# Attention in chunks of 128 tokens, two heads at a time, one chunk shared by both, its probabilities split into two narrow parts; U and V narrowed during the MLP

## The chip, the cores and the metric

The kernel runs on one core of a Trainium2 chip. Its time is the device time of one execution in microseconds (us). The core has a matrix engine (TensorE, PE; its loads of stationary operands are listed as PEld), a vector engine (VectorE, DVE), an activation engine (ScalarE, ACT), a general one (GpSimd, POOL), a queue engine that issues most transfers (SyncE, SP) and sixteen DMA engines. Program order is fixed on each engine ahead of the run; an engine waits where an instruction needs something that another engine or a transfer has not delivered.

## The reference

Four batches of 448 tokens go through three stages. Everything is float32.

```
q_n, k_n = rmsnorm(q, g_q), rmsnorm(k, g_k)          # q, k, v: (4, 12, 448, 64)
attn = softmax(q_n @ k_n.T / 8);  o = attn @ v        # per batch and head
x = o.transpose(0, 2, 1, 3).reshape(4, 448, 768)
xn = layernorm(x) * g_ln
x = x + relu(xn @ w1a) @ w2a                          # 768 -> 3072 -> 768
u = x + (x.T @ U @ V).T                               # U: 448x32, V: 32x448
out = u + relu(u @ w1b) @ w2b
```

## The kernel before

Attention takes the first 335 us, the two MLP passes the rest. The time of the MLP passes is nearly all products that follow one another on PE, in an order written by a planner with costs of its own (`mlps`); smaller work is put between them as side tasks.

Attention works on 48 heads (batch times head), in 24 pairs; n is a head and pr = n // 2 its pair. A head's 448 tokens are four chunks of 112 (CP = 112, NC = 4): a tile of q or k has 112 partitions, and 8 chunks of 64 numbers for the pair. Products keep float32 accuracy by splitting an operand into a narrow high part and the narrow rest: k into k_hi and k_lo, side by side in `kk`; q into q_hi, twice side by side in `qd`, and q_lo in `ql`, which has room for two more columns.

A score is then the sum of two products with the keys of a chunk as the stationary operand: `a1` (k_hi over k_lo, 128 rows) with `bq` (q_hi over q_hi), L503; and `a2` (k_hi, and rows of ones) with `t` (q_lo, and a row with minus the maximum), L504. `a2` needs k_hi on partitions 0 to 63 beside its rows of ones, so a DMA copies a1's upper half into it (L459, the transfer a<-a of the trace). Generators hold the stages of a head:

- `pre_load`, `pre`, `pre_v`, by pair: SP loads q and k (L240); squares and casts on ACT (L290, L316, L319), row sums on DVE (L299), scaling and the low parts on POOL (L297, L313, L318, L321); v comes by ACT's queue.
- `t1` (L438, L448): PE transposes k and q, four blocks each, results pk and pq; ACT casts them into a1 and bq.
- `mx` (L459 to L471): the copy into a2; four products pm, whose row maxima DVE takes (L464); ACT writes minus the maximum into ql.
- `t2` (L479, L481): PE transposes ql, result pt; ACT casts it into t.
- `sc` (L503 to L506): per chunk the two products into one bank ps, and ACT's exponential p. For some chunks p is split (`part`): DVE rounds it to a high part (L494), POOL subtracts (L495).
- `pv` (L521 to L526): p times v with a column of ones, one float32 product of two passes per chunk, or three narrow products where p was split. In all 24 chunks are split, those of heads 6 to 17: chunks 0 and 1.
- `norm` (L535 to L539): DVE copies the sum out, SP writes it to x and the denominators to a scratch.

The main loop has a step per head. In step i it goes round-robin over sc of head i, mx of i + 2, pv of i − 1, t1 of i + 3, t2 of i + 1 and norm of i − 2, four rounds a step, one piece of each per round. A second list (pre, pre_v, layer norm of finished batches, narrowing of the first weights, and at step 4 `load_uv`, which narrows U and V from 64-bit inputs) goes forward by a piece a round. From this order the scheduler fixes each engine's program and the waits. a1 and bq have four buffers by head; a2 has three, taken in turn by head:

```python
a2 = a2s[n % NA2]                                    # before, in t1; NA2 = 3
nc.sync.dma_start(f32(a2[0:D, :]), f32(a1[0:D, :]))  # in mx
```

So the copy for head i + 2 goes into the buffer that head i − 1 read in the step before.

Of the kernel before, what the change touches and what calls it, by code (L numbers as in the profile page):

```python
# [18 lines left out]
P = 128  # L19
CP = 112  # L20
NC = S // CP
DM = H * D
# [11 lines left out]
H0, H2, H1, NV = 6, 18, 18, 2  # L34
# [3 lines left out]
PVY = (0, 1, 2)  # L38
NL = 2
NA2 = 3  # L40
# [7 lines left out]
def build(tc, qkv, gg, g_ln, w1a, w2a, w1b, w2b, u_in, v_in, out):  # L48
    nc = tc.nc
    V, A, PL, PE = nc.vector, nc.scalar, nc.gpsimd, nc.tensor  # L50
    with ExitStack() as es:
# [52 lines left out]
        u4 = const([CP, NC, 4 * R], F32R, "u4")  # L104
        v4 = const([4 * R, S], F32R, "v4")

        def load_ggt(tp):
            gsb = x[B - 1][:CP, 0, :2 * D].rearrange("p (j d) -> p j d", j=2)
            nc.scalar.dma_start(gsb, gg)
            ggt = tp.tile([CP, D], F32, tag="ggt", name="ggt")  # L110
            V.scalar_tensor_tensor(ggt, gsb[:, 0, :], 1.0 / D ** 0.5, gsb[:, 1, :], ALU.mult, ALU.mult)
            return ggt

        def load_uv():
            for src, n, rows in ((u_in, NC * 4 * R, CP), (v_in, S, 4 * R)):
                f = fpool.tile([rows, n], F32, tag="wf", name=f"f{n}")
                src = src.bitcast(U32).rearrange("p (n t) -> p n t", t=2)
                parts = []
                for i in range(2):
                    r = rpool.tile([rows, n // 2, 2], U32, tag="raw", name=f"r{n}_{i}")  # L120
                    nc.sync.dma_start(r, src[:, i * n // 2:(i + 1) * n // 2])
                    parts.append(r)
                yield
                narrow(parts, f)
                yield
                if rows == CP:
                    V.tensor_copy(u4.rearrange("p c r -> p (c r)"), f)
                    part = u4[:, :, 2 * R:3 * R]
                    V.tensor_tensor(part, f.rearrange("p (c r) -> p c r", c=NC)[:, :, 2 * R:3 * R], f32(part), ALU.subtract)
# [96 lines left out]
        def attention(ap, ep, ep2, early, late):  # L226
            NH = B * H
            NP = NH // 2
            kks, vfs, vhs, vls, a2s = [], [], [], [], []
            st = {}  # L230

            def pre_load(pr):
                if pr < NP:
                    b, hp = divmod(pr, H // 2)
                    st["raw", pr] = raw = []
                    for a in range(2):
                        pool, tag, n = ((rpool, "raw", 4), (ap, "rawk", 4))[a]
                        raw.append(pool.tile([CP, 2 * NC, D], F32, tag=tag, name=f"raw{pr}_{a}", bufs=n))
                        q = nc.scalar if pr + a == 0 else nc.sync
                        ins = q.dma_start(raw[a], qkv[b, hp, :, a])  # L240
# [6 lines left out]
            identr = ap.tile([CP, CP], F32R, tag="identr", name="identr")  # L247
            pin(V.tensor_copy(identr, ident[:CP, :CP]))
# [3 lines left out]
            later = ap.tile([CP, D], F32, tag="later", name="later")  # L252
# [180 lines left out]
            def t1(n):  # L433
# [8 lines left out]
                if n == 0:  # L442
                    pin(ins)
# [1124 lines left out]
```

## Time and profile before

| | |
|---|---|
| time, median of 3 runs | 1674.63 us (1674.07 to 1676.15) |
| the profiled execution: its time, its span | 1671.72 us, 1669.6 us |
| PE busy in the span | 1657.2 us (99%) |
| DVE, ACT, POOL busy in the span | 1218.3, 1001.3, 1081.3 us |
| granted PE clock | full (1.0) in every slice |
| attention | 0 to 335 us, the MLP passes from there on |

A busy PE here means that a product is under way by the profile, so a table by stretches tells more than the sum: whether PE has idle time in the stretch, and how much the others have. The chain of waits is followed back from the last instruction, each step to what released it. A group is all instructions of one line, one engine, one pair of tiles.

### The profile page before, as it was taken

What the parts mean: (1) busy time and instruction counts of PE and PEld (TensorE: products, weight loads), DVE (VectorE), ACT (ScalarE), POOL (GpSimd) and SP (SyncE); (2) the same over time, 40 slices, a digit from 0 to 9 for tenths busy, and PEclk for the clock granted to TensorE, in tenths of its full rate; (3) what the DMA queues carried; (4) which work ended last, traced back from release to release, by engine and by line L of the source; (5) the groups of instructions that cost most, each with busy time, mean ns of one, the idle gap of its engine ahead of it and who ended that gap; (6) DMA issues with size and microseconds to landing.
All of it is one profiled execution on the core that took longest, in us unless ns stands there. A gap on an engine that the chain in (4) does not pass through costs nothing.

```text
span 1669.6 us, 24779 instructions
## 1 busy us (share of the span) xinstructions
PE 1657.2 (99%) x8247; PEld 1439.5 (86%) x8247; DVE 1218.3 (73%) x1937; ACT 1001.3 (60%) x2104; POOL 1081.3 (65%) x958
## 2 busy tenths in 40 slices
PE   8999999999999999999999999999999999999999
PEld 6676666599999999999999999999999999999998
DVE  6788787979887887867767786667667854565665
ACT  7887888767878875644544455444445534454541
POOL 5788676459758687755555687555455555776752
PEclk9999999999999999999999999999999999999999
DMA  4444445667665656543544427565757464444432
GB/s 112 114 105 101 131 115 146 195 220 218 217 199 163 193 191 214 183 142 125 160 135 163 158 86 254 192 215 175 225 192 255 157 208 123 144 150 124 152 123 76
DMA packets 134432, 273.42 MB, mean 164 GB/s; under 512 B 37280, under 2 KB 57664, under 8 KB 134304
## 3 DMA queue, kind: packets, MB, share of 16 engines
q1 hardware_dynamic: 112252, 265.24, 50.0%
q10 hardware_dynamic: 22052, 6.59, 1.7%
q8 instruction: 66, 1.08, 0.3%
q14 instruction: 62, 0.51, 0.1%
HBM read 178.80 MB, written 81.96 MB: 156 GB/s over the span
## 4 chain that ended last, share of the span: by engine, by line
PE 92%; DVE 2%; POOL 2%; issue 2%; DMA 1%; ACT 0%; SPq 0%; POOLq 0%; DVEq 0%; ACTq 0%
PE bank L1170 34%; PE bank L1348 32%; PE bank L1292 6%; PE po L521 5%; PE b L1170 3%; PE ps L503 2%; PE b L1292 2%; PE ps L504 2%; PE pm L463 2%; PE b L1348 1%; PE t L1037 1%; PE xt L1027 1%; DVE m L464 1%; PE pk L438 1%; PE pq L448 1%
## 5 line engine op out<-in xcount | busy, mean ns | idle before, releaser
L1348 PE MATMUL bank<-h,w 128*128 128x448 f32 x2607 | 576.0, 366 | 0.0
L1348 PEld LDWEIGHTS bank<-h,w 128*128 128x128 f32 x2607 | 488.4, 188 | 38.4 <-issue 0.4
L1359 DVE TENSOR_TENSOR x<-x,bank 128x448 f32<-128x448 f32 x442 | 270.8, 616 | 189.4 <-PE bank L1348 184.8
L1170 PE MATMUL bank<-xh,w 128*128 128x448 f32 x1122 | 320.2, 367 | 0.0
L844 POOL TENSOR_TENSOR w<-wf,w 128x384 fp32r<-128x384 f32 x201 | 222.7, 1119 | 133.7 <-ACT w L843 132.8
L844 POOL TENSOR_TENSOR w<-s,w 128x384 fp32r<-128x384 f32 x151 | 173.5, 1152 | 154.0 <-ACT w L843 144.0
L1170 PE MATMUL bank<-T,w 128*128 128x448 f32 x1134 | 251.9, 367 | 0.0
L1170 PEld LDWEIGHTS bank<-T,w 128*128 128x128 f32 x1134 | 212.0, 188 | 16.7
L1170 PEld LDWEIGHTS bank<-xh,w 128*128 128x128 f32 x1122 | 210.1, 188 | 17.5 <-issue 0.8
L1170 PE MATMUL bank<-xl,w 128*128 128x448 f32 x561 | 205.1, 366 | 0.0
L843 ACT CAST w<-s 128x384 fp32r<-128x384 f32 x151 | 77.2, 516 | 175.9 <-PE bank L1170 160.9
L843 ACT CAST w<-wf 128x384 fp32r<-128x384 f32 x201 | 101.3, 514 | 100.9 <-PE bank L1170 82.0
L521 PE MATMUL po<-p,vf 112*66 112x448 f32 x336 | 153.2, 539 | 0.6 <-DVE m L464 0.6
L464 DVE TENSOR_REDUCE m<-pm 112x1 f32<-112x448 f32 x192 | 117.8, 617 | 41.3 <-PE pm L463 40.4
L83 DVE SCALAR_TENSOR_TENSOR wf<-wf,raw 128x384 uint32<-128x384 uint32 x180 | 134.9, 756 | 13.7 <-ACT raw L71 5.8
L844 POOL TENSOR_TENSOR w<-raw,w 128x384 fp32r<-128x384 f32 x72 | 81.1, 1143 | 57.4 <-ACT w L843 57.3
L79 ACT ACTIVATE wf<-raw 128x384 f32<-128x384 f32 x180 | 99.1, 552 | 27.9 <-DMA raw<-in_w2a 11.0
L1170 PEld LDWEIGHTS bank<-xl,w 128*128 128x128 f32 x561 | 105.4, 188 | 8.4
L506 ACT ACTIVATE p<-ps 112x448 f32<-112x448 f32 x192 | 104.3, 545 | 4.2 <-PE ps L504 1.9
L1162 DVE SCALAR_TENSOR_TENSOR h<-tm,h 128x448 fp32r<-128x448 f32 x103 | 101.6, 986 | 4.6 <-ACT h L1161 3.8
L71 ACT ACTIVATE raw<-raw 128x384 uint32<-128x384 uint8 x180 | 99.9, 557 | 0.0
L1211 DVE TENSOR_TENSOR tm<-tm,bank 128x448 f32<-128x448 f32 x99 | 61.1, 617 | 44.7 <-PE bank L1170 44.0
(285 smaller groups left out, 3023.8 us busy)
## 6 DMA issues: line engine op xcount, KB each, us to landing
wd<-wf SPq DMA_DIRECT2D x94, 384.0 KB
ws<-w SPq DMA_DIRECT2D x84, 384.0 KB
w<-ws SPq DMA_DIRECT2D x84, 384.0 KB
wf<-wd SPq DMA_DIRECT2D x51, 384.0 KB
raw<-wd SPq DMA_DIRECT2D x48, 384.0 KB
raw<-in_w1b SPq DMA_DIRECT2D x48, 384.0 KB
raw<-in_w2b SPq DMA_DIRECT2D x48, 384.0 KB
raw<-in_w2a SPq DMA_DIRECT2D x44, 384.0 KB
```

What stands on the lines that cost most here:

```text
L71: A.activation(r[:, :, 0], r.bitcast(U8).rearrange("p n (t q) -> p n t q", t=2)[:, :, 0, 3], AF.Copy, scale=1.0 / 32, bias=-31.0 / 64)
L83: V.scalar_tensor_tensor(f, f, 3, r[:, :, 0], ALU.logical_shift_left, ALU.bitwise_or)
L464: ins = V.tensor_reduce(m[:, c:c + 1], pm[:CP, :S], AX.X, ALU.max)
L506: A.activation(p, pb[:CP, :S], AF.Exp)
L521: PE.matmul(po[:QW, :S], vf[:, j, c, :], ps[c], start=(i == 0), stop=(i == NC - 1))
L843: job(A, 520, lambda: A.copy(form(key)[0], src()), ins, ("hi",) + key, [key])
L844: job(PL, 1100, lambda: PL.tensor_tensor(form(key)[1], src(), f32(form(key)[0]), ALU.subtract), [("hi",) + key], key, rel=rel)
L1162: soon(V, 700, lambda: V.scalar_tensor_tensor(at(*key)[:, 1], src(), 0.0, f32(at(*key)[:, 0]), ALU.max, ALU.subtract), [("hh",) + key], ke ...
L1170: PE.matmul(out[:, :S], wt[:, k, :], xt[:, k, :], start=(first and n == 0), stop=(last and n == 8), skip_group_check=True)
L1292: PE.matmul(at(*to)[:, :S], wt[:, e, :], xt, start=(m in "13" and n == 0), stop=(n == 2), skip_group_check=True)
L1348: PE.matmul(at(*key)[:, :S], wt[:, e % 3, :], t, start=(n == 0), stop=(n == 3 * G - 1))
L1359: V.tensor_tensor(x[b][:, e, :], x[b][:, e, :], at(*key)[:, :S], ALU.add)
```

## The change

The 896 tokens of a head pair are seven chunks of 128 (PC = 7). Chunks 0 to 2 are the first head's, 4 to 6 the second's, and chunk 3 holds the last 64 tokens of the first and the first 64 of the second. For chunk 3 the tiles a1, bq and a2 have 64 columns of zeros between the two heads' columns, so that its keys can be taken with the other half zero; its maxima (pm) and its scores (ps) are two products that accumulate in one bank, one for each head, and its p is exponentiated once. A second input layout `vv` holds v in eight slots, the two of the shared chunk with the other head's half zeroed. What was counted by head is now counted by pair, with these numbers before and after: transposes of k and q 384 and 336, of ql 192 and 168; products pm 192 and 192, score products 384 and 384; exponentials 192 and 168; maxima 192 and 168; float32 products of p with v 168 and 140; groups of three narrow ones 24 and 52. Chunk 3 is split in pairs 2 to 21, chunks 2 and 4 also in pairs 3 to 8; the split of chunk 3 is made once and used in a group of three for either head. DVE has 24 copies of 64 columns more, ACT 24 more, POOL 24 small memsets more at the start.

Buffers: a1 has two and bq three, by pair; t has two, by pair, the second in the tile that later holds U and V. Of a2, the first heads of the pairs have two buffers in turn, and all second (odd) heads one, `a2s[1]`, named a21 in the order.

`load_uv` is no longer in attention: it is a side task in the first MLP pass, in three pieces.

The order of the work changes with the pairs. On PE, in a step of an odd head, the last products of attention's rounds; a21 and a22 are buffers of a2 (numbers behind names are those of the tiles), ps, pm, pk and po banks. Before, head 29, with its buffer a22:

```order
L503 MATMUL ps365_3099<-bq_29_2899,a1_29_2850 112x448 [waits Activation_49]
L504 MATMUL ps365_3099<-t2_29_3050,a22_364 112x448 [waits DMAHW2_49]
L463 MATMUL pm366_3106<-a1_31_3026,bq_31_3072 112x448 [waits Activation_49]
L521 MATMUL po367_3109<-p28_0_3012,vf0_348 66x448 [waits DMAHW5_49,DVE_49]
L438 MATMUL pk368_3111<-identr_309,kk16_3007 128x112 [waits PE_49,Pool_49]
L438 MATMUL pk368_3111<-identr_309,kk16_3007 128x112 x3
L503 MATMUL ps369_3127<-bq_29_2899,a1_29_2850 112x448 [waits Activation_49]
L504 MATMUL ps369_3127<-t2_29_3050,a22_364 112x448
L463 MATMUL pm370_3132<-a1_31_3026,bq_31_3072 112x448 [waits DVE_49]
L521 MATMUL po367_3109<-p28_1_3039,vf0_348 66x448
L479 MATMUL pt2371_3136<-identr_309,ql0_366 66x112 [waits DVE_49,Activation_49]
```

After, head 35, from the shared chunk's score on (L558 and L559 are the two score products there, L492 in SP's list the copy):

```order
L558 MATMUL ps400_3414<-bq2_374,a11_368 128x448
L559 MATMUL ps400_3414<-uv0_386,a21_379 128x448 [waits Activation_49]
L507 MATMUL pm401_3417<-a10_366,bq0_370 128x448
L475 MATMUL pk402_3438<-identr_307,kk19_3345 128x128 [waits DVE_49,Pool_49]
L475 MATMUL pk402_3438<-identr_307,kk19_3345 128x128 x3
L558 MATMUL ps403_3451<-bq2_374,a11_368 128x448 [waits PE_49]
L513 MATMUL pm404_3456<-a10_366,bq0_370 128x448 [waits Activation_49]
L596 MATMUL po405_3459<-p17_0_3351,vf1_356 66x448 [waits DMAHW2_49,PE_49]
L558 MATMUL ps406_3468<-bq2_374,a11_368 128x448 [waits DVE_49]
L513 MATMUL pm407_3473<-a10_366,bq0_370 128x448 [waits Activation_49]
L596 MATMUL po405_3459<-p17_1_3377,vf1_356 66x448
L559 MATMUL ps403_3451<-uv0_386,a21_379 128x448 [waits DMAHW3_49]
```

Before, the first product with a22 waits for the copy that was issued in an earlier step, and the later ones for nothing more. Now the second product in this piece is the last of the shared chunk; the last row waits for a transfer into the same a21, and the products and transposes between them are what was moved ahead of it.

On SP, near the end of attention, where wr are first weights and xn, x and sum results. Before:

```order
L980 DMA wr00_4604<-in_w1a 128x768 [waits DMAHW1_49,Pool_49]
L459 DMA a22_364<-a1_41_3893 64x448 [waits DMAHW2_49,PE_49,Activation_49]
L212 DMA xn1_91<-ln1_d5_3903 128x448 [waits DMAHW3_49,DVE_49]
L538 DMA x3_85<-u37_3994 64x448 [waits DMAHW4_49,DVE_49]
L539 DMA sum3_3895<-u37_3994 1x448 [waits DMAHW5_49]
L980 DMA wr01_4606<-in_w1a 128x768 [waits DMAHW6_49,Pool_49]
L459 DMA a20_360<-a1_42_3992 64x448 [waits DMAHW1_49,PE_49,Activation_49]
```

After:

```order
L218 DMA xn1_89<-ln1_d4_3678 128x448 [waits DMAHW5_49,DVE_49]
L1065 DMA wr01_4385<-in_w1a 128x768 [waits DMAHW6_49,Pool_49]
L492 DMA a21_379<-a10_366 64x448 [waits DMAHW7_49,PE_49]
L218 DMA xn1_89<-ln1_d5_3710 128x448 [waits DMAHW0_49,DVE_49]
L625 DMA x3_83<-u37_3794 64x448 [waits DMAHW1_49,DVE_49]
L626 DMA sum3_3729<-u37_3794 1x448 [waits DMAHW3_49]
L492 DMA a22_382<-a11_368 64x448 [waits DMAHW4_49,Activation_49]
```

In both the copies stand between weight loads and results. The copy into a21 after the change waits for PE in its own step, and its source a10 is that of the next pair.

In the program `sc` of head i comes first in a round and `mx` of head i + 2 second, and `mx` issues the copy in its first round. With the one buffer of odd heads the copy for the next pair comes behind the read of chunk 3 and ahead of the reads of chunks 4 to 6, which therefore take the next pair's k_hi in the product with q_lo.

The diff, cut to the parts that are spoken of:

```diff
-H0, H2, H1, NV = 6, 18, 18, 2
+C0, C1, X0, X1 = 2, 22, 3, 9
...
-NA2 = 3
...
         def load_uv():
...
+            t = both()
+            u4, v4 = t[:CP, S:].rearrange("p (c r) -> p c r", c=NC), t[:, :S]
+            uv.extend([u4, v4])
+            for src, rows, at, n in ((u_in, CP, 0, 2 * P), (u_in, CP, 2 * P, 2 * P), (v_in, P, 0, S)):
...
+                    r = lpool.tile([rows, n // 2, 2], U32, tag="lt", name=f"r{rows}_{at}_{i}")
+                    nc.sync.dma_start(r, src[:, at + i * n // 2:at + (i + 1) * n // 2])
+                    raws.append(r)
+                for _ in range(3):
+                    yield
+                narrow(raws, f)
                 yield
...
+            def halved(pr):
+                return (2, 3, 4) if X0 <= pr < X1 else (3,) if C0 <= pr < C1 else ()
...
+            a1s, bqs, a2s, t2s = [], [], [], []
+            for lst, nm, n in ((a1s, "a1", 2), (bqs, "bq", 3)):
+                for i in range(n):
+                    t = ep2.tile([P, 2 * S + HC], F32R, tag=f"{nm}{i}", name=f"{nm}{i}")
+                    PL.memset(f32(t[:, S:S + HC]), 0.0)
+                    lst.append(t)
+            for i, j in enumerate((0, 1, 0)):
+                t = ap.tile([P, S + HC], F32R, tag=f"a2{i}", name=f"a2{i}")
                 PL.memset(f32(t[D:QW, :]), 1.0)
+                PL.memset(f32(t[:QW, 0:HC] if j else t[:QW, S:]), 0.0)
                 a2s.append(t)
+            t2s.append(ap.tile([P, 2 * S], F32R, tag="t2", name="t2"))
+            t2s.append(both())
             qls = []
...
+            def a2_of(n):
+                pr, j = divmod(n, 2)
+                return a2s[1] if j else a2s[2 * (pr % 2)]
+
+            def cols(n):
+                o = n % 2 * (S + HC)
+                return slice(o, o + S)
+
+            def keys(c, j):
+                o = c * P if c < 3 or not j else c * P + HC
+                return slice(o, o + P)
...
-                a2 = a2s[n % NA2]
-                st["ab", n] = (a1, bq, a2)
+                if not j:
+                    st["ab", pr] = (a1s[pr % 2], bqs[pr % 3])
+                cs = range(NC) if not j else range(NC, PC)
+                for nm, src, t in (("pk", kk, st["ab", pr][0]), ("pq", qd, st["ab", pr][1])):
+                    pt = bank(nm)
+                    for c in cs:
+                        o = (c - cs[0]) * P
+                        PE.transpose(pt[:, o:o + P].bitcast(F32R), src[:, c].rearrange("p a d -> p (a d)"), identr)
+                    hold = pin if n == 0 or nm == "pq" and n in (1, 3) else lambda ins: ins
+                    if not j:
+                        hold(A.copy(t[:, 0:S], pt[:, :S]))
+                        hold((A.copy if nm == "pk" else V.tensor_copy)(t[:, S + HC:S + P], pt[:, S:S + HC]))
+                    else:
+                        hold(A.copy(t[:, S + P:2 * S + HC], pt[:, 0:S - HC]))
+                    if nm == "pk":
+                        yield
...
             def mx(n):
-                a1, bq, a2 = st["ab", n]
-                nc.sync.dma_start(f32(a2[0:D, :]), f32(a1[0:D, :]))
-                m = ap.tile([CP, NC], F32, tag="m", name=f"m{n}", bufs=2)
-                for c in range(NC):
-                    pm = bank("pm")
-                    PE.matmul(pm[:CP, :S], bq[:, c * CP:(c + 1) * CP], a1, start=True, stop=True)
-                    ins = V.tensor_reduce(m[:, c:c + 1], pm[:CP, :S], AX.X, ALU.max)
+                pr, j = divmod(n, 2)
+                a1, bq = st["ab", pr]
+                ql = st["tok", pr][1]
+                a2 = a2_of(n)
+                to = slice(HC, S + HC) if j else slice(0, S)
+                nc.sync.dma_start(f32(a2[0:D, to]), f32(a1[0:D, cols(n)]))
+                if not j:
+                    st["m", pr] = ap.tile([P, PC], F32, tag="m", name=f"m{pr}", bufs=2)
+                m = st["m", pr]
+
+                def top(c, pm):
+                    ins = V.tensor_reduce(m[:, c:c + 1], pm[:, :S], AX.X, ALU.max)
                     if n == 2:
                         pin(ins)
-                    if c < NC - 1:
+
+                def turned(c, d):
+                    A.mul(ql[:, c:d, D:D + 1], m[:, c:d].unsqueeze(2), -1.0)
+
+                if j:
+                    pm = st.pop(("pm", pr))
+                    PE.matmul(pm[:, :S], bq[:, keys(3, 1)], a1[:, cols(n)], start=False, stop=True)
+                    top(3, pm)
+                    turned(0, NC)
+                    yield
+                for c in range(NC, PC) if j else range(3):
+                    pm = bank("pm")
+                    PE.matmul(pm[:, :S], bq[:, keys(c, j)], a1[:, cols(n)], start=True, stop=True)
+                    top(c, pm)
+                    if c < PC - 1:
                         yield
-                pr, j = divmod(n, 2)
-                ql = st["tok", pr][1]
-                A.mul(ql[:, j * NC:(j + 1) * NC, D:D + 1], m.unsqueeze(2), -1.0)
+                if j:
+                    turned(NC, PC)
+                else:
+                    st["pm", pr] = pm = bank("pm")
+                    PE.matmul(pm[:, :S], bq[:, keys(3, 0)], a1[:, cols(n)], start=True, stop=False)
 
...
             def sc(n):
-                a1, bq, a2 = st.pop(("ab", n))
-                t = st.pop(("t2", n))
-                st["p", n] = ps = []
-                st["hl", n] = hl = []
+                pr, j = divmod(n, 2)
+                a1, bq = st["ab", pr]
+                a2, t = a2_of(n), t2s[pr % 2]
+                t = t[:QW, j * S:(j + 1) * S]
...
+                def score(pb, c, start=True, stop=True):
+                    k = keys(c, j)
+                    o = k.start - j * S
+                    PE.matmul(pb[:, :S], a1[:, k], bq[:, cols(n)], start=start, stop=False)
+                    PE.matmul(pb[:, :S], a2[:QW, o:o + P], t, start=False, stop=stop)
+
+                def expd(pb, c):
+                    ps[c] = p = ap.tile([P, S], F32, tag="pf", name=f"p{pr}_{c}", bufs=NC + 2)
+                    A.activation(p, pb[:, :S], AF.Exp)
+
+                if j:
+                    part(2)
+                    pb = st.pop(("pb", pr))
+                    score(pb, 3, start=False)
+                    expd(pb, 3)
+                    yield
+                for c in range(NC, PC) if j else range(3):
+                    if c in (5, 6):
+                        part({5: 3, 6: 4}[c])
                     pb = bank("ps")
-                    cs = slice(c * CP, (c + 1) * CP)
-                    PE.matmul(pb[:CP, :S], a1[:, cs], bq, start=True, stop=False)
-                    PE.matmul(pb[:CP, :S], a2[:QW, cs], t[:QW], start=False, stop=True)
-                    p = ap.tile([CP, S], F32, tag="pf", name=f"p{n}_{c}", bufs=NC + 2)
-                    A.activation(p, pb[:CP, :S], AF.Exp)
-                    ps.append(p)
-                    if c < NC - 1:
+                    score(pb, c)
+                    expd(pb, c)
+                    if c < PC - 1:
                         yield
+                if not j:
+                    st["pb", pr] = pb = bank("ps")
+                    score(pb, 3, stop=False)
 
...
-                    if c >= m:
-                        PE.matmul(po[:QW, :S], vf[:, j, c, :], ps[c], start=(i == 0), stop=(i == NC - 1))
+
+                def times(po, s, c, first, last):
+                    if c in hl:
+                        ph, pl = hl[c]
+                        w = s - 2
+                        PE.matmul(po[:QW, :S], vh[:, w, :], ph, start=first, stop=False)
+                        PE.matmul(po[:QW, :S], vl[:, w, :], ph, start=False, stop=False)
+                        PE.matmul(po[:QW, :S], vh[:, w, :], pl, start=False, stop=last)
                     else:
-                        ph, pl = hl[c]
-                        PE.matmul(po[:QW, :S], vh[:, j, c, :], ph, start=False, stop=False)
-                        PE.matmul(po[:QW, :S], vl[:, j, c, :], ph, start=False, stop=False)
-                        PE.matmul(po[:QW, :S], vh[:, j, c, :], pl, start=False, stop=(i == NC - 1))
-                    if i in PVY:
+                        PE.matmul(po[:QW, :S], vf[:, s, :], ps[c], start=first, stop=last)
+
...
-                if i == 4:
-                    ln.append(load_uv())
...
+                if (layer, pair, c) == (0, 1, 2):
+                    side.append((even, 4, "uv", load_uv()))
...
+    vv[:, :, :, :NC - 1] = v[:, :, :, :NC - 1]
+    vv[:, :, :HC, NC - 1] = v[:, :, :HC, NC - 1]
+    vv[:, :, HC:, NC] = v[:, :, HC:, NC - 1]
+    vv[:, :, :, NC + 1:] = v[:, :, :, NC:]
```

## Rows read from the trace of the kernel before

**Rows 1.** Stretches; us; busy us (count) PE, PEld, DVE, ACT, POOL; clock; DMA; GB/s.
```profile
0.00:40.00 40.00, 35.57 (x209) 26.59 (x209) 27.82 (x60) 29.59 (x71) 20.00 (x33) 1.00 0.43 113
40.00:335.00 295.00, 290.55 (x1436) 182.63 (x1435) 236.78 (x448) 244.16 (x574) 209.81 (x178) 1.00 0.49 130
335.00:668.00 333.00, 333.00 (x1642) 307.94 (x1641) 280.67 (x390) 250.86 (x484) 248.01 (x206) 1.00 0.64 201
700.00:750.00 50.00, 50.00 (x256) 46.30 (x255) 33.19 (x53) 26.00 (x54) 29.29 (x27) 1.00 0.48 153
```

**Rows 2.** Chain of waits, steady attention: start us, us, engine, result, line, count.
```profile
59.17 0.29 PE pk L438 x4
59.46 0.27 PE ps L503
59.73 0.21 PE ps L504
59.93 0.20 PE pm L463
60.14 0.75 PE po L521 x2
60.89 0.22 PE pt L479 x4
61.11 0.26 PE ps L503
```

**Rows 3.** Time line of PE in a split chunk: start us, us, instruction.
```profile
81.90 0.37 PE L524 MATMUL po<-xl,vh 112*66 112x448 f32 x1
82.10 0.36 PE L525 MATMUL po<-xl,vl 112*66 112x448 f32 x1
82.30 0.36 PE L526 MATMUL po<-xl,vh 112*66 112x448 f32 x1
82.50 0.36 PE L503 MATMUL ps<-bq,a 128*112 128x448 f32 x1
```

**Rows 4.** Groups, 40 to 335 us: shapes, count; busy us, mean ns; idle before.
```profile
L464 DVE TENSOR_REDUCE m<-pm 112x1 f32<-112x448 f32 x171 | 105.3, 617 | 38.0 <-PE pm L463 37.2
L506 ACT ACTIVATE p<-ps 112x448 f32<-112x448 f32 x179 | 97.5, 546 | 4.2 <-PE ps L504 1.9 <-PE pm L463 0.9 <-ACT ln_mu L172 0.5
...
L504 PEld LDWEIGHTS ps<-t,a 66*112 66x112 f32 x178 | 31.5, 177 | 8.7 <-issue 4.6 <-ACT p L506 1.0 <-ACT t L481 0.8
...
L495 POOL TENSOR_TENSOR xh<-p,xh 112x448 fp32r<-112x448 f32 x12 | 14.1, 1180 | 1.9 <-DVE xh L494 0.7 <-DVE ss L301 0.6 <-DVE ln L148 0.4
...
L494 DVE TENSOR_REDUCE xh<-p 112x448 fp32r<-112x448 f32 x12 | 7.3, 611 | 1.4 <-ACT p L506 1.4
```

**Rows 5.** Page, groups of the whole span: the MLP's loads of 128 columns.
```profile
L1348 PEld LDWEIGHTS bank<-h,w 128*128 128x128 f32 x2607 | 488.4, 188 | 38.4 <-issue 0.4
```

**Rows 6.** Time line of POOL at the start; in brackets its idle time before.
```profile
3.07 0.21 POOL L278 MEMSET ql<- 112x16 f32 x3
6.05 1.28 POOL L380 TENSOR_TENSOR raw<-raw,ggt 112x512 f32<-112x512 f32 x1 [2.76 <-DVE identr L248]
...
15.46 1.04 POOL L362 TENSOR_TENSOR raw<-raw,sy 112x512 f32<-112x512 f32 x1 [1.41 <-DVE sy L149]
...
20.01 1.27 POOL L297 TENSOR_TENSOR raw<-raw,later 112x512 f32<-112x512 f32 x1
```

**Rows 7.** Time line of SP: issues of the copy for the second score product.
```profile
81.92 0.47 SPq L459 DMA_DIRECT2D a<-a  x1
...
88.09 0.46 SPq L459 DMA_DIRECT2D a<-a  x1
```

**Rows 8.** DMA, 81.9 to 85.9 us in 40 slices: busy share in tenths.
```profile
DMA  0000000000055998520000100000003698893000
```

**Rows 9.** Chain of waits in attention's tail: the two longest transfers.
```profile
284.95 3.75 DMA a<-a
...
303.94 6.16 DMA wr<-in_w2a
```

More of the change, by code (lines that the diff above doesn't have):

```diff
@@ L296, in pre @@
                     yield
-                pin(PL.tensor_tensor(raw[0], raw[0], over(later, [CP, n8, D], 1), ALU.mult))
+                pin(PL.tensor_tensor(raw[0], raw[0], over(later, [P, n8, D], 1), ALU.mult))
                 for a in range(2):
@@ L318, in pre @@
                 PL.tensor_tensor(kk[:, :, 1, :], raw[1], f32(kk[:, :, 0, :]), ALU.subtract)
-                pin(A.copy(qd, over(raw[0], [CP, n8, 2, D], 2)))
+                pin(A.copy(qd, over(raw[0], [P, n8, 2, D], 2)))
                 yield
@@ L368, in high @@
                     else:
-                        pin(A.copy(qd, over(raw[pr][0], [CP, n8, 2, D], 2)))
+                        pin(A.copy(qd, over(raw[pr][0], [P, n8, 2, D], 2)))
                 def low(E, pr, a):
@@ L396, in first_two @@
                 low(PL, 0, 0)
-                pin(PL.tensor_tensor(raw[1][0], raw[1][0], over(later, [CP, n8, D], 1), ALU.mult))
+                pin(PL.tensor_tensor(raw[1][0], raw[1][0], over(later, [P, n8, D], 1), ALU.mult))
                 pre_load(3)
@@ L475, in t2 @@
                 ql = st["tok", pr][1]
+                t = t2s[pr % 2]
                 yield
+                if not j:
+                    yield
                 pq = bank("pt2")
-                for c in range(NC):
-                    PE.transpose(pq[:QW, c * CP:(c + 1) * CP].bitcast(F32R), ql[:, j * NC + c], identr)
-                t = ap.tile([P, S], F32R, tag="t2", name=f"t2_{n}", bufs=T2 + 1)
-                ins = A.copy(t[:QW], pq[:QW, :S])
+                cs = range(NC) if not j else range(NC, PC)
@@ new lines, in pv @@
+                if not j:
+                    if n:
+                        yield
+                    po = st["po", n] = bank("po")
+                    for c in range(3):
+                        times(po, c, c, c == 0, False)
+                        if c < 2:
+                            yield
+                else:
+                    times(st["po", n - 1], 3, 3, False, True)
+                    po = st["po", n] = bank("po")
+                    times(po, 4, 3, True, False)
+                    order = (5, 6, 4) if 4 in hl else (4, 5, 6)
+                    for i, c in enumerate(order):
+                        yield
+                        times(po, c + 1, c, False, i == 2)
```

179 lines of the change are left out of this document (82 added, 97 removed).

## The prediction

> **What bounds the kernel now.** I read the table by stretches first. TensorE (PE) is busy 290.55 us of the 295 from 40 to 335 us, the attention after its start, and 333.00 of 333 and 50.00 of 50 in the two stretches of the MLPs, at full granted clock (2.4 GHz) everywhere [rows 1]. What PE is spared in attention therefore shortens the program, and what another engine is spared shows only as far as PE waits for it: 40.00 − 35.57 = 4.43 us before 40 us and 295 − 290.55 = 4.45 after. The other engines have room: DVE 236.78, ACT 244.16, POOL 209.81 of the 295. In the chain of waits the products of a round then follow one another [rows 2]: a product in one pass starts 0.20 us after the one before, a product of p with v 0.75 (F32, two passes), and a block of four transposes 0.29 or 0.22, after which the next product takes 0.26 or 0.27 instead of 0.20.
>
> **The sum, part by part.**
>
> *More p split.* In place of one F32 product a split chunk has three narrow ones. In the row of a split chunk the first starts at 81.90 us and the product after the third at 82.50, so 0.60 [rows 3], against 0.75. The change has 52 groups of three instead of 24: a shared chunk's split serves a product for either head (20 pairs × 2), and six pairs have two more. So 28 × (−0.15) = −4.2 us. Chunks that are split number 32 instead of 24, each with a DVE pass of 0.611 and a POOL pass of 1.18 us [rows 4]: +4.9 on DVE, +9.4 on POOL. Against that DVE has 24 maxima fewer of 0.617 (−14.8), ACT 24 exponentials fewer of 0.546 (−13.1) [rows 4], and POOL's token work 448 columns a partition instead of 512. No engine beside PE gets fuller, so I put the cover at whole. What it costs if it isn't: a split that comes 0.2 late in each of 32 chunks would be +6.
>
> *Fewer transposes.* k and q have seven blocks a pair instead of eight, with 128 columns instead of 112: 336 for 384, and 168 for 192 of the third kind. A block of four pk costs 0.29 plus the 0.06 to 0.07 that the next product is late, so 0.35, or 0.088 each; of pt 0.22 + 0.05 = 0.27, or 0.067 [rows 2]. If an instruction costs the same at 128 columns: 48 × 0.088 = 4.2 us less for k and q, and 24 × 0.067 = 1.6 for the third kind. If the cost goes by columns, 7 × 128 = 8 × 112 and nothing is won. The pk blocks (128 rows of result) and the pt blocks (66) have the same moving columns and unlike times, so columns alone don't set it. I take −4.2: k and q by instruction, the third kind by column. Bounds −5.8 and 0.
>
> *As many products as before.* Maxima and scores: the shared chunk has one product per head into one bank, so 8 a pair of either, 192 and 192 + 192 as before, and 192 chunks of p with v. They now load 128 stationary columns where there were 112. The load of 112 columns takes 177 ns and that of 128 in the MLP 188 [rows 4, 5], both under the 0.20 at which products start, so I put it at 0. The Trainium skill, "TensorE: Matmul & The Clock Gate", section "LDWEIGHTS (loading the stationary operand)", has a load grow with its columns; here the rows agree in the sign, but 66 columns [rows 3], 112 [rows 2] and 128 (333.00 / 1642 = 0.203 in the MLP [rows 1]) go by at the same pace, which leaves the load hidden. Were it not hidden, the 576 products would pay 11 ns each, the fourth rival.
>
> *Start.* The first chain runs through POOL and ACT: instructions of 1.28, 1.04 and 1.27 us on 512 columns [rows 6]. With 448 an eighth goes: about six of them, 6 × 1.2 × 0.125 = −0.9; I take −0.8. There are 24 small memsets more on POOL, of some 0.1 us by the 3 × 0.07 of the row at 3.07 us, so 2.4 us, and POOL waits 2.76 us before its first real work at 6.05, which hides them; uncovered they'd cost up to 2.2. Bounds −1.5 and +2.2.
>
> *U and V narrowed later.* In attention this takes DVE, ACT, POOL work and four SP loads away and so, with the relief above, part of PE's 4.45 us of idle: −1, bounds −4.45 and 0. In the MLPs the same work stands beside a PE at 50.00 of 50 with DVE at 33.19 and ACT at 26.00 [rows 1]; the MLP's products stand in the same order as before. I put it at 0; if h is late once for each of its pieces, three to six waits under 0.8 us, up to +5.
>
> *The wait that is new.* Head n's second score product reads k_hi from a copy (a<-a) on partitions 0–63. Before, three buffers went round by head, the copy was issued two steps ahead and had a step (6.2 us, the distance of the copies issued at 81.92 and 88.09 us [rows 7]) to land. Now all odd heads have one buffer, and the copy for the next odd head stands, in the program, behind only the first read of this one. So PE's chunk-4 product waits for the landing of a copy that was released in the same step, by chunk 3's product. Behind that product on PE: chunk 5's, eight transposes, the score of chunk 6, and ACT's exponentials and casts wait for these. The work between release and wait, from the order and the durations above: pm 0.20, four pk 0.355, ps 0.20, pm 0.20, po 0.76, ps 0.20, pm 0.20, po 0.76 = 2.88 us. A product ends 0.37 after its start [rows 3], 0.17 beyond the 0.20 that is counted for it, and the two hand-overs to and from the queue I estimate at 0.09 together, so 2.62 are left from issue to landing. The copy issued at 81.92 [rows 7] has its packets on the queues from 83.0 to 83.7, so lands some 1.8 to 2.2 after issue [rows 8]. Margin 0.4: no stall while the queues are quiet. But in the tail the copy took 3.75 us, and a 384-KB load 6.16 [rows 9]. In SP's order the copies of the last four pairs stand behind weight loads or a string of normalised rows. I price those four at 3.75 − 2.62 = 1.13, rounded up for the 6.16 to 1.25 each: +5. Bounds 0 (all land in 2.2) and 4 × (6.16 − 2.62) = +14.
>
> The Trainium skill, "DMA: Bandwidth & Descriptors", section "Issuing engines are not separate DMA queues", says that transfers share the same 16 engines and interleave, whoever issues them. The rows on the tail copy agree (3.75 us against about 2), and it is what speaks against this change: the margin is only as good as the quiet of the queues.
>
> Sum: −4.2 − 4.2 − 0.8 − 1 + 5 = −5.2 us. Against the profiled execution (1671.72 us around a span of 1669.6) that is 1666.5. The median of the runs shown is 1674.63, 2.9 above that execution, so I carry the difference over: **1669.6 us** after rounding the difference to −5. About 0.2%, 3.35 us, is what a measurement of this kernel can tell from none.
>
> **Rivals.**
>
> *A, slower: every pair's copy is late.* The copy lands later than 2.62 us because x and sum of the even head (SP L538, L539 before) and the next raw loads are under way. Two pairs have longer cover, 22 pay. Without stalls the sum is −10.2, so it turns slower than before from 10.2 / 22 = 0.46 us a pair, a landing at 3.08. At 3.3: 22 × 0.68 = +15, so +4.8, 1679.4. For it: the loaded 3.75. Against: rows 8 show the quiet case in mid-attention, with 0.4 of margin.
>
> *B, no change: transposes by column, the tail stalls.* −4.2 (splits) − 0.8 − 1 + 5 = −1: 1673.6. For it: the same moving data in fewer blocks. Against: the pk and pt blocks above.
>
> *C, clearly faster: no stalls.* −10.2: 1664.4. For it: the tail's PE had waits of its own already (the stretch lacks 4.45 us in all), and a late copy may coincide with one of these. Against: the 3.75.
>
> *D, the stationary load is not hidden.* 576 × 11 ns = +6.3, with the forecast's −5 gives +1.3: 1676. For it: the 188 ns beside 0.20. Against: the equal pace at 66 and 128 columns.
>
> **How the numbers follow.** Forecast 0.42, B 0.25, C 0.18, A 0.12, D 0.03. Own range of the forecast: transposes at −5.8 and stalls of 2 give 1666, transposes at −2.5 gives 1671.3. The range that holds 8 in 10 goes from beyond C, with all idle regained (another −3.4): 1661.0, to near A, with stalls of 14 in the tail alone (+9 on the forecast): 1678.0. Faster by over 0.2%: the forecast without its upper tail (0.40), C (0.18), a little of B: 0.59. Within 0.2%: most of B, D and the forecast's tail: 0.27. Slower: A and bits of B and D: 0.14.
>
> **What would show it.** In the profile after: 140 F32 products of p with v and 52 groups of three narrow ones; transposes of k and q at 336 with a block of four still near 0.29; PE busy from 40 us on about 8 to 9 us shorter up to the first MLP product. In the list of PE's waits, the line of the second score product ends waits on "DMA a<-a", four of them, all in the last 60 us, 1 to 2 us each, and none between 40 and 270. The copy from issue to landing 2.1 to 2.2 in the middle. MLP stretches at PE 100% with the narrowing of U and V inside. Wrong if the waits on the copy come in every pair (A), if a block of pk takes 0.33 (B), or if products start 0.21 apart in attention (D).

## The result, and the profile after

The changed kernel takes 1686.46 us, median of 6 runs (1683.65 to 1690.36); the kernel before, 6 runs beside them, 1675.39. The ratio of the two is 1.0068 (95% interval 1.0051 to 1.0085). The change makes the kernel slower by some 11 us, where 5 us faster were forecast and 1678 was the upper end of the range. The profiled execution took 1685.71 us, 14 more than that of before.

All of it lies in attention. Below are the stretches of the changed kernel, columns as in [rows 1]. Line numbers (L559) are those of the kernel of the run that is shown, so the same line of code has other numbers in other runs:

```profile
0.00:40.00 40.00, 34.80 (x202) 26.67 (x202) 26.31 (x61) 28.30 (x72) 21.89 (x52) 1.00 0.41 117
40.00:335.00 295.00, 276.98 (x1351) 182.27 (x1352) 217.59 (x420) 216.46 (x549) 204.54 (x196) 0.98 0.45 120
335.00:668.00 333.00, 333.00 (x1619) 302.12 (x1618) 277.62 (x397) 256.86 (x499) 239.57 (x200) 1.00 0.64 203
700.00:750.00 50.00, 50.00 (x248) 46.23 (x247) 37.58 (x65) 30.73 (x67) 37.79 (x35) 1.00 0.57 185
```

The MLP's stretches are as before, PE full. From its first product to the last the MLP lasts 1331.3 us, before 1331.1. Its first product starts at 348.67 us instead of 334.58, 14.1 later. From 40 to 335 us PE was busy 290.55 us [rows 1] and is now 276.98, at a mean clock of 0.98. DVE, ACT and POOL are less busy too (up to the first MLP product 255.9, 255.9 and 227.1 us, before 264.2, 273.3 and 229.4). PE waits more, and these are its longest waits (from the list of PE's waits in the changed kernel: line, what was waited for, us in total, times, longest):

```profile
PE ps L559 <- DMA a<-a: 10.4, 11, 2.7
PE po L594 <- POOL w L552: 2.9, 3, 2.0
PE pm L513 <- DVE u L622: 2.5, 1, 2.5
PE ps L558 <- DVE u L622: 1.2, 1, 1.2
```

The first is the wait that is new. The list counts idle time only. Taken from the start of one product to the start of the next, with the 0.1 us by which the product after such a wait is late, there are 14 waits for the copy and 14.5 us. One of the middle ones, in the time line of PE (start us, us, instruction, idle time before):

```profile
87.31 0.37 PE L559 MATMUL ps<-uv,a 66*128 66x448 f32 x1
...
87.72 0.45 PE L475 MATMUL pk<-identr,kk 128*128 128x128 f32 x4
88.01 0.44 PE L558 MATMUL ps<-bq,a 128*128 128x448 f32 x1
88.28 0.36 PE L513 MATMUL pm<-a,bq 128*128 128x448 f32 x1
88.48 0.91 PE L596 MATMUL po<-p,vf 128*66 128x448 f32 x2
...
89.63 0.91 PE L596 MATMUL po<-p,vf 128*66 128x448 f32 x2
91.41 0.68 PE L559 MATMUL ps<-uv,a 66*128 66x448 f32 x2 [0.87 <-DMA a<-a]
```

Chunk 3's product reads the buffer at 87.31. The work up to the wait is what the prediction added up: four pk in 0.29 and the next product after 0.27, as in [rows 2] with 112, so a block of 128 columns costs no more; and L559 could have started at about 90.4. It starts at 91.41. The transfers issued around it, in the time line of all engines (SPq and ACTq are the queues of SP and ACT):

```profile
86.89 0.38 ACTq L451 DMA_DIRECT2D vf<-in_vv  x1
...
87.30 0.52 ACTq L451 DMA_DIRECT2D vf<-in_vv  x1
...
87.71 0.46 SPq L492 DMA_DIRECT2D a<-a  x1
...
88.26 0.66 SPq L625 DMA_DIRECT2D x<-u  x1
...
88.98 0.44 SPq L626 DMA_DIRECT2D sum<-u  x1
```

The copy (L492) is issued at 87.71, on time. The last of its sixteen parts lands 3.66 us later; [rows 8] had some 2.1. It is not the write of x behind it that makes the difference, but the two loads of v ahead of it, which ACT issues (L451), as E2 shows.

The trace of the kernel before already had such copies. Of the 38 that it issues from 36 to 279 us, 11 land later than 2.62 us, and the one issued at 127.89, with four reads of a scratch by SP (from 125.27 on) and two loads of v by ACT (at 127.20 and 127.59) ahead of it, after 4.41. [rows 8] shows one of the quiet ones.

Then there is something that no term of the sum had. At the three longest waits (2.69 us up to 283.90, 2.71 up to 300.79, 2.46 up to 330.40) the granted clock falls from 2.4 to 1.2 GHz (0.50) for some 3.4 us: it does so 1.7 and 1.9 us after PE has started again behind the first two, and 0.4 us before the end of the third, which is a wait for DVE's copy of a result (u) and not for the transfer. Stretches inside, columns as above:

```profile
286.00:289.00 3.00, 3.00 (x8) 1.80 (x7) 0.84 (x3) 1.93 (x6) 2.97 (x4) 0.50 0.00 0
...
303.00:306.00 3.00, 3.00 (x8) 1.92 (x7) 1.36 (x3) 2.69 (x8) 1.60 (x3) 0.50 0.51 158
330.00:333.00 3.00, 2.60 (x8) 1.38 (x9) 2.85 (x5) 1.98 (x5) 3.00 (x4) 0.50 0.65 192
```

PE is busy in nearly all of these 3 us and does half the work. That is about 1.7 us lost each time, 5 in all. In the profile of the kernel before the clock was 1.00 throughout attention and the MLP.

### The profile page after: what moved, and what is told of

Read it like the earlier page. It is cut to its first block, busy times and chain, and to the rows that moved or that the text cites. A ratio compares the mean times of both kernels' runs of the same rounds, so it can differ in the third digit from the quotient of the medians.

```text
span 1683.9 us, 24766 instructions
## 1 busy us (share of the span) xinstructions
PE 1657.1 (98%) x8203; PEld 1446.5 (86%) x8203; DVE 1207.5 (72%) x1951; ACT 988.0 (59%) x2122; POOL 1081.6 (64%) x996
## 4 chain that ended last, share of the span: by engine, by line
PE 93%; DMA 3%; DVE 2%; ACT 1%; issue 1%; POOL 0%; ACTq 0%; DVEq 0%; POOLq 0%
PE bank L1255 34%; PE bank L1433 32%; PE bank L1377 6%; PE po L596 4%; PE b L1255 3%; DMA a<-a 3%; PE ps L559 2%; PE ps L558 2%; PE b L1377 2%; PE pm L513 1%; PE b L1433 1%; DVE m L498 1%; PE t L1122 1%; PE xt L1112 1%; PE warm L257 1%
## 5 line engine op out<-in xcount | busy, mean ns | idle before, releaser
L498 DVE TENSOR_REDUCE m<-pm 128x1 f32<-128x448 f32 x168 | 103.3, 618 | 42.7 <-PE pm L513 41.5
L596 PE MATMUL po<-p,vf 128*66 128x448 f32 x280 | 128.8, 546 | 0.0
L563 ACT ACTIVATE p<-ps 128x448 f32<-128x448 f32 x168 | 89.5, 548 | 36.5 <-PE ps L559 30.6
L1247 DVE SCALAR_TENSOR_TENSOR h<-tm,h 128x448 fp32r<-128x448 f32 x103 | 98.0, 952 | 5.6 <-ACT h L1246 5.3
L558 PE MATMUL ps<-bq,a 128*128 128x448 f32 x192 | 99.2, 518 | 1.6 <-DVE u L622 1.2
```

Source lines behind the costliest of these rows:

```text
L498: ins = V.tensor_reduce(m[:, c:c + 1], pm[:, :S], AX.X, ALU.max)
L558: PE.matmul(pb[:, :S], a1[:, k], bq[:, cols(n)], start=start, stop=False)
L596: PE.matmul(po[:QW, :S], vf[:, s, :], ps[c], start=first, stop=last)
```

## The experiments

The first table shows where a pair's time goes. It has the time from the first transposed block of k of one pair to that of the next, in undisturbed pairs, from the traces:

| layout, groups of three narrow products in the pair | us a pair |
|---|---|
| before, none | 12.87 |
| before, four | 12.28 |
| after (runs with the late copy below), none | 12.69 |
| after, two | 12.40 |
| after, four | 12.10 |

The second has the medians, each against the runs of the kernel before on the same chip, and the start of the MLP in the run's profile:

| run | median us | ratio, 95% interval | first MLP product, us |
|---|---|---|---|
| before (three runs) | 1674.63 | | 334.58 |
| the changed kernel | 1686.46 | 1.0068 (1.0051 to 1.0085) | 348.67 |
| E1 late copy | 1680.25 | 1.0017 (1.0004 to 1.0029) | 339.72 |
| E2 loads of v later | 1673.28 | 0.9986 (0.9976 to 0.9997) | 336.02 |
| E3 late copy, no split | 1669.58 | 0.9960 (0.9944 to 0.9975) | 334.45 |
| E4 before, U and V later | 1675.04 | 0.9999 (0.9985 to 1.0012) | 334.91 |
| E5 late copy, split in pairs 2 to 9 | 1668.91 | 0.9958 (0.9944 to 0.9972) | 329.39 |
| E6 changed, split in pairs 2 to 9 | 1681.12 | 1.0031 (1.0016 to 1.0046) | 345.26 |
| E7 loads of v later, split in pairs 2 to 9 | 1669.78 | 0.9964 (0.9950 to 0.9977) | 331.87 |
| E8 before, more split | 1690.68 | 1.0085 (1.0071 to 1.0099) | 354.05 |
| E9 all three | 1665.74 | 0.9944 (0.9931 to 0.9958) | 328.72 |

**E1, the copy behind the last read.**

```diff
-                nc.sync.dma_start(f32(a2[0:D, to]), f32(a1[0:D, cols(n)]))
+
+                def copied():
+                    nc.sync.dma_start(f32(a2[0:D, to]), f32(a1[0:D, cols(n)]))
+
+                if not j or n < 4:
+                    copied()
...
                 for c in range(NC, PC) if j else range(3):
+                    if c == PC - 1 and n >= 4:
+                        copied()
```

> The changed kernel, but from head 4 on the copy of k_hi for an odd head is issued in the last round of its step, behind all four reads of the one buffer, so it has two steps to land (the chunks 4 to 6 then read their own pair's k_hi). Theory 'copy': the waits for the copy (14.5 us start to start, with the refill of 0.1 behind each) and two of the three drops of the clock behind the long ones (1.7 us each) go, 1686.5 - 17 = 1669 to 1671. Rival 'other engines': PE waits for the copy only because DVE, ACT and POOL are late in any case, and the waits move to the row maxima, the splits and u: 1680 to 1686. Rival 'wider blocks': products with 128 stationary columns are slower than with 112; the waits go, yet PE's own work is no less than before, 1675 or more.

No wait for the copy is left, and undisturbed pairs take what the sum said. But the time fell by 0.5% only, half of what "copy" forecast; 1680.25 lies at the edge of "other engines", so each of the two holds in part. "Wider blocks" is out: a pair takes 12.69 us, which is less than 12.87. Up to pair 11 the run is ahead of before by 3.0 us (135.75 against 138.77); the next two pairs lose 4.9. There PE waits for a split:

```profile
156.30 0.36 PE L600 MATMUL po<-w,vl 128*66 128x448 f32 x1
156.50 0.36 PE L566 MATMUL ps<-uv,a 66*128 66x448 f32 x1
160.03 0.64 PE L601 MATMUL po<-w,vh 128*66 128x448 f32 x1 [3.16 <-POOL w L559]
160.46 0.58 PE L599 MATMUL po<-w,vh 128*66 128x448 f32 x1
160.83 0.58 PE L600 MATMUL po<-w,vl 128*66 128x448 f32 x1
161.21 0.58 PE L601 MATMUL po<-w,vh 128*66 128x448 f32 x1
```

And this is POOL at that time (its time line: the last part of the layer norm of a finished batch, ln_d, with the token work of a coming pair, ql and raw, between):

```profile
152.68 1.13 POOL L352 TENSOR_TENSOR ql<-raw,qd 128x448 fp32r<-128x448 f32 x1
153.78 1.14 POOL L328 TENSOR_TENSOR raw<-raw,later 128x448 f32<-128x448 f32 x1
154.88 1.13 POOL L225 TENSOR_TENSOR ln_d<-x,ln_mu 128x448 f32<-128x448 f32 x1
155.98 1.83 POOL L344 TENSOR_TENSOR raw<-raw,sy 128x448 f32<-128x448 f32 x2
157.77 1.12 POOL L225 TENSOR_TENSOR ln_d<-x,ln_mu 128x448 f32<-128x448 f32 x1
158.85 1.12 POOL L559 TENSOR_TENSOR w<-p,w 128x448 fp32r<-128x448 f32 x1
```

DVE's half of the split was done by 153.8; POOL's (L559) starts at 158.85, at the end of a row of instructions without a gap. Behind the wait of 3.16 us the products start 0.37 to 0.38 us apart instead of 0.20. It is the clock again: the granted clock is 0.50 for 6.8 us from 159.4 on, which costs another 3.4 us.

**E2, the loads of v out of the way.**

```diff
+                if pr > 1:
+                    yield
+                    yield
                 for j in range(2):
```

> The changed kernel with the copy where it is; only the two loads of v for the next pair are issued two rounds (some 3 us) later, so that they are not under way when the copy is issued. Theory 'v ahead': the copy then lands 2.1 to 2.3 us after its issue in the middle of attention, as in the three pairs where no load of v stood ahead of it (2.10, 2.14, 2.10), and the eleven waits of 0.1 to 1.1 us there go (8 us with refills): 1678 to 1680, with the two long waits of the tail left. Rival 'raw and x': it is the write of x right behind the copy, or the loads of q and k, that slow it: landing stays at 2.8 to 3.8 and the time at 1685 to 1687. Rival 'margin too small': even at 2.2 us the waits stay at about half, 1682.

The loop at the end of the cut issues the two loads of v. The result is better than expected: 1673.28, 0.8% below the changed kernel. SP's issues and PE in the same step as above:

```profile
85.62 0.46 SPq L495 DMA_DIRECT2D a<-a  x1
86.17 0.55 SPq L628 DMA_DIRECT2D x<-u  x1
86.77 0.43 SPq L629 DMA_DIRECT2D sum<-u  x1
87.29 0.84 SPq L246 DMA_DIRECT2D raw<-in_qk  x2
```

```profile
87.54 0.91 PE L599 MATMUL po<-p,vf 128*66 128x448 f32 x2
87.94 0.92 PE L562 MATMUL ps<-uv,a 66*128 66x448 f32 x2
88.70 0.46 PE L478 MATMUL pq<-identr,qd 128*128 128x128 f32 x4
```

The write of x stands 0.55 us behind the copy as it did, the loads of q and k 1.67; the copy now lands after 2.14 us, and the product that reads it (L559 above, L562 here) follows the one before it without a wait. Of the 18 copies into this buffer from 36 to 257 us, 15 land within 2.08 to 2.54 us. The DMA engines' share in tenths, in 0.1 us from the issue of the copy, first in the changed kernel and then here:

```profile
DMA  0012457999999999979599694113297446699998
```

```profile
DMA  0000000000058899357997930019979087999998
```

In the changed kernel the engines fill up from 0.2 us on and are full by 0.8, with the loads of v (1056 of the 1388 packets in these 4 us are on the queue of ACT's loads; here none of 365). This settles "v ahead" against "raw and x" and "margin too small". Two waits for the copy are left (2.1 and 1.1 us, in the tail behind a weight load), and behind the longer one the clock is at 0.50 for 3.4 us.

E2 keeps all 52 groups of narrow products and two waits for the copy, and yet it is 7 us faster than E1, which has no wait for the copy. In the profiles its longest wait for a split is 1.3 us where E1's is 3.2, and it loses 1.7 us to the clock where E1 loses 3.4. What a late split costs thus depends on what else POOL and DVE have to do at that moment; these edits also shift the order of other instructions on those engines, and no run takes that apart.

**E3, E5, E6: which splits cost.** E3 is E1 with `C0, C1, X0, X1 = 0, 0, 0, 0`; E5 is E1, and E6 the changed kernel, with `C0, C1 = 2, 10`.

> As the run with the late copy, and with no p split at all (52 groups of three narrow products become 52 products in float32). By the term of the sum, 52 x 0.15 = 7.8 us more of PE work, less the waits of products for a split (2.9 us in the changed kernel): 5 to 8 us above the run with the late copy, 1674 to 1678. Rival 'split hidden or paid for by waits': no more than 2 us above it.

> The late copy, with p split in pairs 2 to 9 only (40 groups instead of 52: those whose scores come before the layer norm of the first batch occupies POOL and DVE). Theory 'split behind the layer norm': with the splits of all pairs the run with the late copy lost some 10 us from pair 12 on against the run without any split and won 3.7 us before it; so this keeps the gain and loses the waits: 1665 to 1667, 3 to 4 us below the run without splits (1669.6). Rival 'tail': the tail ends at its own time whatever comes before it (the run without splits was 4.2 us ahead at the last pair and only 0.1 at the first MLP product), 1669 to 1670. Rival 'splits cost anywhere': 1672 to 1676.

> The changed kernel, its copy in the old place, with p split in pairs 2 to 9 only. Theory: the waits for the copy stay (14.5 us and two drops of the clock), those for late splits go: 1679 to 1682, 5 to 8 below the changed kernel. Rival 'copy alone': the waits for splits lay beside those for the copy, so no more than 2 us: 1684 to 1686.

Without any split the kernel is 10 us faster than with 52 groups, where the term of the sum made it 7.8 slower. My expectation failed, and its rival ("no more than 2 us above") had no gain of this size in mind either. By pairs the traces part. Up to pair 11 the splits win 3.8 us (E1 is there at 135.75, E3 at 139.52); from there to pair 23 they lose 10.3 (303.46 against 296.97), the 3.4 of the clock included. E5 keeps the gain and drops the loss: it is at pair 23 at 294.52 us, 2.5 ahead of E3. In the median it is only as fast as E3 (0.9958 and 0.9960, intervals that overlap), which is the time that "tail" gave. E6 shows the same on the changed kernel: leaving out the late splits takes the ratio from 1.0068 to 1.0031, some 6 us, within what its theory said, with the copy's waits still there (10.6 us of idle time in its list). Of these 6 us some 3.4 are clock, for E6's profile has one drop (from 299.7 on) where the changed kernel's has three.

The profile of E3 shows how the tail can take back what was won: it is 4.2 us ahead of before at pair 23, and 0.1 at the first MLP product. Its chain of waits there:

```profile
311.55 6.45 DMA wr<-in_w1a
...
318.09 0.55 ACT wf L79
318.64 0.48 ACT uv L542
...
319.16 0.47 PE ps L566
```

It is a load of first weights (6.45 us), its narrowing on ACT (wf), and behind that in ACT's order the cast of t (uv) that PE waits for. PE's idle time up to 319.16 is 2.2 us, and the clock is at 0.50 for 3.4 us from 319.6 on, another 1.7: together nearly all of the 4.1 us lost. But this is one chain, I took nothing away there to test it, and the profiled execution (1676.16) is the slowest of E3's seven and the only one whose mean granted clock was under 1.000. So it isn't shown that the tail is why E5 and E3 have the same median.

**E4, U and V alone.** The kernel before with the new `load_uv`, as a side task of the MLP.

> The kernel before with one part of the change alone: U and V are narrowed as a side task of the first MLP pass, in three pieces, and no longer at step 4 of attention. By the term of the sum: -1 us (0 to -2), 1673.5 to 1675.5, PE still at 100% in the MLP. Rival 'MLP pays': +2 to +5 us with PE idle beside the narrowing. Rival 'attention is freed': -3 to -4.5 us.

The ratio is 0.9999, so there is no change that can be seen; the interval (0.9985 to 1.0012, or −2.5 to +2.0 us) is wide enough to hold the −1 of the sum. At pair 5 attention is 1.26 us ahead (63.83 against 65.09), at pair 23 0.5, at the first MLP product 0.3 behind. What it frees early is given back. In the list of PE's waits nothing of U and V stands. "MLP pays" and "attention is freed" lie outside the interval.

**E7, both repairs, the copy in its place.** `C0, C1 = 2, 10` on E2.

> The changed kernel with the loads of v two rounds later and p split in pairs 2 to 9 only; the copy in its old place. Theory: both repairs add up but for the two waits for the copy that remain in the tail (2 and 3 us with a drop of the clock): 1666 to 1669. Rival 'tail': 1671 to 1673, as with the loads of v moved alone.

The median is 1669.78, beyond the end of the theory's range and under the rival's. The repairs add up in part: leaving out the late splits brings 3.5 us here, some 6 on the changed kernel (E6) and some 10 with the late copy (E1 against E5).

**E8, more split in the kernel before.** `H1 = 42`: one chunk of heads 18 to 41 as well.

> The kernel before with more p split and nothing else: one chunk of every head from 18 to 41 as well (24 groups of three more, 48 instead of 24). Theory 'split behind the layer norm': 24 x 0.15 = 3.6 us less PE work, and products that wait for POOL while it does a layer norm, of the same size or more, so 1675 to 1680, with waits on POOL's split in the rows. Rival, my prediction's own term: the splits are covered, -3.6: 1671.

It is 0.85% slower, more than the theory said, and my own term is refuted here: with 24 groups more the kernel is 14 us slower, where the term made it 3.6 faster. Not all 14 us can be put down to the splits. In the profile the granted clock is 0.50 three times, for 6.8 us from 14.5 on, 6.8 from 195.4 on and 3.4 from 304.6 on, some 8.5 us lost, and with the first of these the run is 2.6 us behind at the start, before any added split. The waits are not on POOL's split as I expected; they come by way of DVE. Part of the chain:

```profile
193.27 1.15 POOL ln_d L219
...
194.45 0.04 DVE ln_d L222
...
195.05 0.63 DVE m L464
...
195.72 0.71 PE pm L463
```

POOL's ln_d of the layer norm is late; DVE's next instruction waits for it, the row maximum (m) stands behind that on DVE, and PE waits for the bank. That the added splits are what makes ln_d late is argued from POOL's fixed order, not shown.

**E9, late copy, later loads of v, more split but only in pairs 2 to 9.** `C0, C1, X0, X1 = 2, 10, 2, 10` on both edits.

> Late copy, loads of v two rounds later, and p split in pairs 2 to 9 only, in all of them with the chunks 2 and 4 too (48 groups instead of the 40 of the run with the late copy and these pairs). Theory: no wait for a copy, no split behind the layer norm, and 8 x 0.15 = 1.2 us less PE work: 1667 to 1668.5. Rival 'tail': 1668.5 to 1670, as the run with 40 groups, since the end of attention is set by DVE, the weight loads and ACT there. Slower than that run (over 1671) if more splits are late also before the first layer norm.

The median is 1665.74, the ratio 0.9944: it is the fastest run, below the lower end of what I expected, and faster than both kernels. (Its interval overlaps with those of E3, E5 and E7.) Its stretches and its longest waits:

```profile
40.00:328.72 288.72, 282.67 (x1368) 185.43 (x1368) 222.78 (x434) 226.18 (x563) 190.68 (x178) 1.00 0.49 133
335.00:668.00 333.00, 333.00 (x1641) 307.99 (x1640) 281.14 (x394) 252.01 (x485) 242.71 (x202) 1.00 0.64 200
```

```profile
PE pq L478 <- DVE m L506: 1.6, 2, 1.2
PE pk L478 <- POOL kk L349: 1.1, 1, 1.1
PE ps L568 <- DVE u L632: 1.1, 1, 1.1
```

There is no copy, no split and no drop of the clock among them. What is left are waits of 1.2 us or less, most of them for DVE, and the start: in the first 40 us PE is busy for 35.54.

## Why the prediction was wrong

- *Fewer transposes, −4.2*: this was right. A pair takes 12.87 − 12.69 = 0.18 us less, or 4.3 for 24 pairs, and the pk block of 128 columns takes 0.29 as that of 112 did. Rival B (by column) is out, and so is D.
- *More p split, −4.2*: the size of a group was right (12.69 − 12.10 = 0.59, four times 0.15). The step that failed is "I put the cover at whole". I compared sums over 295 us, 209.81 for POOL, and these mix quiet pairs with those in which a finished batch's layer norm keeps POOL without a gap. Before, the 24 splits lay all in quiet pairs; the change puts 12 of the 20 shared chunks behind the first layer norm. Leaving these out is worth some 6 us in the changed kernel (E6), 3.5 with the loads of v later (E2 against E7) and some 10 with the late copy (E1 against E5), part of it clock. My bound of +6 for late splits came nearest and did not go into the range. The sum also left out that a split makes its pair halve v: a cast on ACT and a subtraction on POOL (0.56 us in the mean), in 20 pairs instead of 6. E5 and E6 take away this work together with the splits, so what either costs alone is open.
- *The wait that is new, +5*: the mechanism was right, and so were the cover of 2.9 us, the 2.62 left of it, the quiet landing of 2.1 and the price of a late copy: one that landed after 3.66 us cost about 1.0. The two hand-overs that I put at 0.09 took 0.07 in the wait shown above. The step that failed is "no stall while the queues are quiet", with the four pairs of the tail alone priced. I took one quiet row for the middle of attention, where 11 of 38 copies of the kernel before landed too late for the new margin; and I looked for what is ahead of the copy in SP's order, while the two loads of v are issued by ACT. They come less than a microsecond ahead in most pairs. The waits cost 14.5 us, past my bound of +14, and came in 14 pairs and not in four. This is rival A, which I gave 0.12, with other transfers than those I named, and with landings of mostly 2.8 to 3.9 us in the middle. The Trainium skill, "DMA: Bandwidth & Descriptors", section "Issuing engines are not separate DMA queues", was cited for just this; the trace agrees, 3.66 against 2.14 us in the same step, and I did not follow it to ACT's queue.
- *The clock*: the sum had no term for it. It cost 5 us at three long waits.
- *U and V, −1*, and *the start, −0.8*: E4 measures 0 for U and V, with an interval that doesn't exclude −1. The start was not separated: pair 4 begins 1.6 to 2.0 us earlier in the runs with the late copy, some 0.7 of it by the transposes.
- *The MLP at 0*: this was right.

By terms, the profiles make it −8.5 of PE work, +14.5 for the copy, +5 for the clock and some +3 for late splits beside the clock, 14 in all, where 14.1 were measured. The start and what of before's own waits went are not in this sum, so its agreement is good to a few us only. The medians lie 11 us apart.

Two of the prediction's sums are slightly off, and nothing here rests on them: transposes at −5.8 with stalls of 2 give 1665, not 1666, and 9 above the forecast is 1678.6, not 1678.0.

## What to carry to other kernels

A transfer on the critical path competes with all queues: list what every engine issues in the microseconds ahead of it, not what stands before it on its own. Cover by an engine that isn't the bound is read in the stretch where the work will stand; its mean over a phase hides a stage in which it is full. And a wait of a few microseconds on TensorE can cost more than itself, when the granted clock falls at it, as it did here for 3.4 to 6.8 us.

## What was not expected of the hardware

The granted clock fell to 1.2 GHz within attention in most of the profiles with long waits, and the length of the wait alone doesn't tell when. It fell at waits of 2.69, 2.71 and 2.46 us in the changed kernel, 3.16 in E1, 2.06 in E2, 2.24 in E3 and 1.56 in E6, but not at one of 1.97 in the changed kernel (up to 163.75 us). It stayed there for 3.4 us, or 6.8 in E1 and twice in E8. The profiles of the kernel before, E4, E5, E7 and E9 have no such fall in attention.

The MLP, with the same 6605 products from its first to its last and PE at 100% and full clock in the records, lasted 1331.1 to 1333.4 us in nine profiles, and 1336.1 and 1335.9 in those of E1 and E3, whose products start 0.2023 us apart in the mean instead of 0.2016. What sets it stays open. The runs of the kernel before spread as much (1671.73 to 1681.42). The clock has a part in that: the 26 of 55 with a mean granted clock of 1.000 have a median of 1674.1 us, the 13 with 0.997 or less 1677.8. Differences of less than about 5 us between the whole spans of single profiles thus say nothing; the readings above rest on medians and on attention alone.
